# Sigmoid attention and a token mixer on one core: nearly all matrix work in 64x64 tiles, with the PSUM banks and the order of steps written out

## The chip, the core and the metric

The kernel runs on one core of one Trainium2 chip. A core has five engines with an instruction queue each: TensorE (PE, matrix products, with weight loads shown apart as PEld), VectorE (DVE), ScalarE (ACT), GpSimd (POOL) and SyncE (SP, which here issues the DMAs). TensorE writes into PSUM, eight banks of 512 float32 for each of 128 partitions; VectorE and ScalarE copy from there to SBUF. The metric is the time of one execution in microseconds of the device.

## The reference

```python
scores = scale * np.matmul(q, k.transpose(0, 1, 3, 2)) - np.log(S)
attn = 1.0 / (1.0 + np.exp(-scores))
attn_out = np.matmul(attn, v)                  # batch 8, 12 heads, 448 tokens, 64 wide
x = attn_out.transpose(0, 2, 1, 3).reshape(B, S, H * D)        # 8 x 448 x 768
wq = x @ w_q                                    # 768 -> 64
wk = x @ w_k
W_tok = scale * np.einsum('bsd,btd->bst', wq, wk)
mixed = np.einsum('bst,btd->bsd', W_tok, x)
out = np.maximum(mixed, 0.0) @ w_out            # 768 x 768
```

Inputs and output are float32; the products run in bfloat16 with float32 sums.

## The kernel before

**Units.** Four heads of one batch are a quad: 24 quads, three to a batch. Tokens are split into seven groups of 64 (`NI`, `NP`). Two batches are a window; their output rows are computed together.

**Attention.** For each quad, q and k are loaded, cast to bfloat16 and transposed so that the 64-wide head lies along the partitions. There are several ways to do that, and a letter for each: small 64x64 transposes on TensorE (`q`, `k`), whole 128x128 ones (`a`, `b`), or transposes of 32x32 blocks on VectorE after GpSimd has swapped quarters of the tile (`c`, `d`, `arrange`), or VectorE alone (`r`, `s`, `z`, `quadrants`). A step `S` (`scores`, L329 is its sigmoid) makes the scores of one token group of the keys, in four 64x64 tiles and two PSUM banks, and ScalarE turns them into attention weights. A step `P` (`values`) multiplies these with v and sums over the seven groups in two banks; after the seventh, the sum is copied to the x tile `xt` (L351).

**Mixer.** `x` transposes a quad of x to token rows (`tr_x`, small or whole), `W` adds one of six parts of the wq and wk product (`mlp_wqk`), `N` transposes wk (`mlp_wkn`), `U` forms the wk-x product (`mlp_tmp`, or `mlp_tmp_tiled`), `M` the mix and its ReLU (`mlp_mix`). With `mlp_mix` associated this way, no 448x448 token matrix is formed.

**Output.** `O` is a part of an output block. In windows 1 and 2 (`TW`) it is `out_pair`: two token groups of 64, 48 products in 64x64 tiles, four parts, two banks. In windows 0 and 3 it is `out_chunk`, with whole 128x128 products of a token pair into one bank, or `out_halves`. The tiled blocks need w_out in both halves of the partitions; the second copy is made by DMAs from SBUF to SBUF (`C`, L920). `D` issues the store of a finished block.

**What sets the order.** The order is written out: `PLAN` is a string with one letter for each step, and every engine's instructions stand in its queue in that order, under `manual_schedule`. Loads are issued on SP in the order of `ORDER`, at most six ahead of the casts; GpSimd casts them in that order, except those marked for VectorE, which wait `LAG` score steps. Some loads wait for a given product (`BEHIND`). PSUM banks come from a list of free pairs, first in, first out (`bank2`, `bank1`, `release`). All four 64x64 tiles of a group run in TensorE together; where the next group has another tile shape, the shape changes. Letters `F` are dummy products of 128x512 in the first quads.

Of the kernel before, what the change touches and what calls it, by code (L numbers as in the profile page):

```python
# [9 lines left out]
F32 = mybir.dt.float32  # L10
# [7 lines left out]
def kernel(  # L18
# [49 lines left out]
    free2 = [0, 1, 2, 3]  # L68
    halves = []

    def bank2():
        n = free2.pop(0)
        return n, pairs[n], pairs16[n]

    def bank1():
        if halves:
            n, b = halves.pop(0)
        else:
            n, b = free2.pop(0), 0
            halves.append((n, 1))  # L80
        return (n, b), pairs[n][:, b], pairs16[n][:, b]

    def release(fb):
        if isinstance(fb, int):
            free2.append(fb)
        elif (fb[0], 1 - fb[1]) in halves:
            halves.remove((fb[0], 1 - fb[1]))
            free2.append(fb[0])
        else:
            halves.append(fb)  # L90
# [5 lines left out]
    spare = singles.tile([P, 8], F32)  # L96
# [3 lines left out]
    xts = [singles.tile([P, 2, 512], BF16, name=f"xt{n}") for n in range(2 * NJ)]  # L100
    wqks = [singles.tile([P, 512], BF16, name=f"wqk{n}") for n in range(2)]
    wq2s = [singles.tile([P, S], BF16, name=f"wq2{n}") for n in range(2)]
# [25 lines left out]
    def xt(u, j):  # L128
        return xts[u % 2 * NJ + j]


    TW = (1, 2,)
# [3 lines left out]
        "FSSFFFFKSSSqFFSSkFFSSDPpSFpPSPPPqSSkPSPPSSpPpPSabSXSPpSSPSPr"  # L136
        "PXpSPSSFSszSWWWWXSPWWPSppPNSpPSqkSSUSXSMSPpSMPpSppPSSqkSPpPP"
        "SPSWWcPSPXSWWSSdMWXSWSPpPpSpNPPSqSkSUSxSMSPpppSppSCPoSOSMSOo"
        "SqCkSOoCMSpPpSDpPcPSPSdoOSSocOSLLDLSXSdLLSLPPpSppPSPSoOSoSNC"
        "xSOcDSUSPPDSPprCdPpSPpSsPpPDPSPSoPSXoSMSOoSzLLxSLLLLScSoXoSM"  # L140
        "ppDpSPpDCSpdPSOOcSpppSpPSPPSONMSYOSxSOdOSpPpPpSSDPPoOSxSUcSL"
        "LLDdSSLLLppPSppPPSoSoMSOcSOSDdPpPPSPMoPSoPmOSOScdOoSxoSDOSON"
        "oSxSOOSSUpSppPSMcpPpLLLSLpPSPdLLpDDPPSOpoSxoSOmocDSoMSodooDS"
        "NOSoSOSPPPPDtcpSppOoSMoSODoSoSdMOOSPPScpppPSOPmoOSoxoDSdOSoS"
        "OLLSLLLSLoSooNxScoPppxSpdPSPPoSODDSoSOSOOSxoSOSTppPpPSpPpPpP"
        "mPppmmWWWWWWyyINiiitiiIMiiMMIiioOoOoOOoOoOoOOOO"
    )
    PLAN = "".join(PLAN)
    KIND = ["a"] + [t for t in PLAN if t in "qacer"]
# [6 lines left out]
    def arrange(n, eng):  # L156

        arranged.add(n)
        if KIND[n] in "er":
            return  # L160
# [21 lines left out]
    def load1(n, nm, eng, m):  # L182
        u, j = quads[n]
        if KIND[n] in "cer" and nm != "v":
# [19 lines left out]
    def cast1(n, nm, e):  # L204
        if KIND[n] in "cer" and nm != "v":
# [48 lines left out]
    moves = []  # L254

    def move():
        n, m = moves.pop(0)
        for g in range(2):
            for h in range(2):
                own, other = 64 * g + 32 * h, 64 * g + 32 * (1 - h)  # L260
                nc.sync.dma_start(
                    out=qk[n][other : other + 32, h].rearrange("p t i n -> p (t i n)"), in_=m[own : own + 32, 1 - h],
                )

    def tr(n, nm, kind):
# [9 lines left out]
        if kind in "cdef":  # L275
# [5 lines left out]
            if kind in "ef":  # L281
                if t == 0:
                    moves.append((n, p_mv.tile([P, 2, 2 * S], BF16, tag="mv", name="mv")))
                nc.vector.transpose(out=moves[-1][1][:, t].bitcast(F32), in_=w)
# [5 lines left out]
        if kind in "abh":  # L290
            transposes_whole(ps[:, t], t16, slice(0, NI))
        else:
            transposes(ps[:, :, t * S : (t + 1) * S], t16, slice(0, NI))
# [41 lines left out]
    def values(n, i, tail, eng):  # L335
# [10 lines left out]
        if i == NI - 1:  # L346
            if tail:
                for h in range(2):
                    COPY["vs"[h]](out=xt(u, j)[:, h, 0:S], in_=ps[:, h, 0:S])  # L349
# [621 lines left out]
```

## Time and profile before

| what | value |
|---|---|
| median of 3 runs | 185.96 us (185.79 to 186.71) |
| span of the profiled execution | 184.0 us |
| own time of that execution beside its span | not given on the page; the median is 1.96 us above the span |
| TensorE busy | 174.7 us, 3662 products |
| ScalarE busy | 162.7 us, 168 of its 209 instructions are sigmoids |
| VectorE busy | 133.1 us |
| GpSimd busy | 124.3 us |
| moved by DMA | 48.51 MB, 264 GB/s mean |

How to read the profile: an engine's busy time is the union of its instructions' times. Products on TensorE overlap, and their ends are modelled, so a busy TensorE is not one at its peak. In a row of the timeline, the first number is the start in microseconds from the start of the span, the second the time from the first start to the last end of a run of like instructions, `xN` their count. In a view by stretches, each engine has its busy time and, in brackets, the instructions that ended there; PEclk is the share of its full clock that TensorE was granted. In a view of groups, the busy time and the mean length in ns stand behind the bar, then the idle time before them and what ended it. In a view of waits: total us, times, longest.

### The profile page before, as it was taken

Reading aid. Unit: us, or ns where it says so; the run is one execution under the profiler, and the core shown is the slowest. Engines: PE = TensorE matmul, PEld = TensorE weight load, DVE = VectorE, ACT = ScalarE, POOL = GpSimd, SP = SyncE. Lnnn points to the kernel's source line nnn. Section 1 sums busy time; section 2 is a strip of 40 time slices with the busy share of each in tenths; the row PEclk is TensorE's granted clock in tenths of the full one; section 3 lists DMA queues with packets and bytes.
Section 4 is the critical chain, followed back from the end, with each engine's and each line's share of the span. In section 5 each row is a group of like instructions: output and inputs, shape, how many; then the busy total and the mean of one; then the engine's idle time right before and its main releaser. Section 6 shows DMA issues by size and latency. Waiting matters only on the chain.

```text
span 184.0 us, 8547 instructions
## 1 busy us (share of the span) xinstructions
PE 174.7 (95%) x3662; PEld 115.3 (63%) x3662; DVE 133.1 (72%) x209; ACT 162.7 (88%) x209; POOL 124.3 (68%) x171
## 2 busy tenths in 40 slices
PE   7888989999999999999999999999999999999990
PEld 7344545554545464565555778667898878869660
DVE  3334878788798887899797788587678476686820
ACT  4699999999999999999999989999999989876230
POOL 1458799995799899779999996999999920000000
PEclk9999999999999999999999999999999999999998
DMA  5999999969999999989987984798997443422596
GB/s 177 356 385 383 328 361 360 379 229 304 331 357 326 298 289 332 344 291 315 337 298 232 349 284 145 221 321 226 352 309 226 106 125 89 116 62 60 133 237 171
DMA packets 26085, 48.51 MB, mean 264 GB/s; under 512 B 3968, under 2 KB 19968, under 8 KB 26048
## 3 DMA queue, kind: packets, MB, share of 16 engines
q1 hardware_dynamic: 25888, 47.79, 79.9%
q8 instruction: 28, 0.46, 1.1%
q10 hardware_dynamic: 160, 0.20, 0.4%
q14 instruction: 9, 0.07, 0.1%
HBM read 35.78 MB, written 11.01 MB: 254 GB/s over the span
## 4 chain that ended last, share of the span: by engine, by line
PE 78%; ACT 14%; issue 3%; DVE 2%; ACTq 0%
PE banks L119 73%; ACT at L329 13%; PE banks L122 6%; DVE xt L351 1%; DVE mx L480 1%; ACTq L661 0%; DVE ld L680 0%; DVE wqk L426 0%; ACT xt L349 0%; ACT wq L428 0%; ACT ld L678 0%; DVE zeros L716 0%; ACTq L329 0%; ACTq L678 0%; ACTq L428 0%
## 5 line engine op out<-in xcount | busy, mean ns | idle before, releaser
L329 ACT ACTIVATE at<-banks 128x896 bf16<-128x896 f32 x168 | 141.2, 932 | 4.8 <-PE banks L119 4.3
L119 PE MATMUL banks<-wout,mx 64*64 64x384 bf16 (+2 forms) x954 | 68.5, 323 | 0.0
L119 PE MATMUL banks<-qk 64*64 64x448 bf16 x672 | 61.8, 358 | 2.0 <-ACT at L329 1.3
L119 PEld LDWEIGHTS <-mx 64*64 64x64 bf16 (+1 forms) x954 | 41.1, 105 | 14.4 <-issue 5.1
L119 PE MATMUL banks<-at,v 64*64 64x448 bf16 x672 | 45.6, 351 | 0.2
L119 PEld LDWEIGHTS <-qk 64*64 64x64 bf16 x672 | 25.5, 105 | 21.4 <-issue 12.6
L209 POOL CAST qk<-ld 128x896 bf16<-128x896 f32 x28 | 33.6, 1210 | 5.4 <-DVE qk L280 1.4
L119 PEld LDWEIGHTS <-v 64*64 64x64 bf16 x672 | 22.7, 106 | 9.2 <-issue 2.4
L351 DVE CAST xt<-banks 128x896 bf16<-128x896 f32 x19 | 20.7, 1088 | 10.2 <-PE banks L119 9.8
L480 DVE TENSOR_SCALAR mx<-banks 128x1024 bf16<-128x1024 f32 (+2 forms) x21 | 21.1, 1011 | 3.9 <-PE banks L119 3.1
L219 POOL CAST v<-ld 128x896 bf16<-128x896 f32 x23 | 21.6, 954 | 1.9 <-DMA ld<-in_v_dram 1.6
L168 POOL COPY qk<-qk 32x448 uint32<-32x448 uint32 x28 | 16.4, 587 | 1.6
L280 DVE STREAM_TRANSPOSE qk<-qk 128x448 f32<-128x448 f32 x28 | 17.4, 629 | 0.0
L171 POOL COPY qk<-swap 32x448 uint32<-32x448 uint32 x28 | 15.9, 568 | 1.6
L165 POOL COPY swap<-qk 32x448 uint32<-32x448 uint32 x28 | 15.7, 562 | 1.7
L560 DVE COPY o<-banks 128x768 f32<-128x768 f32 x11 | 10.5, 952 | 5.7 <-PE banks L119 4.1
L122 PEld LDWEIGHTS <-xt 64*64 64x64 bf16 (+1 forms) x528 | 10.9, 107 | 3.6 <-issue 2.4
L119 PE MATMUL banks<-xt,wqk 64*64 64x448 bf16 (+1 forms) x138 | 12.7, 350 | 0.1
L122 PE MATMUL banks<-ident,xt 64*64 64x64 bf16 (+1 forms) x528 | 12.4, 198 | 0.1
L395 DVE COPY xn<-banks 128x1024 bf16<-128x1024 bf16 (+1 forms) x14 | 9.0, 648 | 3.3 <-PE banks L122 2.7
L119 PE MATMUL banks<-wqk,tmp 64*64 64x256 bf16 (+1 forms) x72 | 8.9, 298 | 0.1
L119 PE MATMUL banks<-wq,tmp 64*64 64x256 bf16 (+1 forms) x72 | 9.0, 300 | 0.0
(73 smaller groups left out, 159.1 us busy)
## 6 DMA issues: line engine op xcount, KB each, us to landing
ld<-in_q_dram SPq DMA_DIRECT2D x24, 448.0 KB, 5.8
ld<-in_v_dram SPq DMA_DIRECT2D x24, 448.0 KB, 5.7
ld<-in_k_dram SPq DMA_DIRECT2D x23, 448.0 KB, 6.2
out_dram<-o SPq DMA_DIRECT2D x42, 192.0 KB, 4.8
ld<-in_moe_w_out_dram SPq DMA_DIRECT2D x6, 384.0 KB, 6.2
out_dram<-ld SPq DMA_DIRECT2D x11, 192.0 KB, 2.8
wout<-wout SPq DMA_DIRECT2D x12, 96.0 KB, 6.7
out_dram<-ld SPq DMA_DIRECT2D x4, 96.0 KB, 2.4
```

The source lines that it names most:

```text
L119: products.append(nc.tensor.matmul(*args, **kw))
L122: products.append(nc.tensor.transpose(*args, **kw))
L165: eng.tensor_copy(out=z[lo], in_=w[hi, 0])
L168: eng.tensor_copy(out=w[hi, 0], in_=w[lo, 1])
L171: eng.tensor_copy(out=w[lo, 1], in_=z[lo])
L209: COPY[e](out=f[:, :, "qk".index(nm)].rearrange("p e i d y -> p e y i d"), in_=ld.pop((nm, n)).rearrange("p (y i e d) -> p e y i d", y=2, ...
L219: COPY[e](out=t16.rearrange("p i b d -> p b i d"), in_=ld.pop((nm, n)).rearrange("p b (i d) -> p b i d", i=NI),)
L280: nc.vector.transpose(out=qk[n][:, t].rearrange("p t i n -> p (t i n)").bitcast(F32), in_=w)
L329: nc.scalar.activation(at, sc[:, :, 0:S], ACTF.Sigmoid, bias=attn_bias, scale=attn_scale)
L351: COPY[eng](out=xt(u, j)[:, :, 0:S], in_=ps[:, :, 0:S])
L480: nc.vector.tensor_scalar(dst, ps, moe_scale, 0.0, ALU.mult, ALU.max)
L560: COPY["s" if act else "v"](out=o, in_=ps[:, :, 0:NB])
```

## The change

- Every window is tiled: `TW` holds all four, and the output blocks are all `out_pair`, 28 blocks of 48 products. `out_halves`, `mlp_tmp_tiled` and the special last chunk are gone. The mixed tile `mx` holds 12 x 224 columns a batch instead of 12 x 256, without overlap; for that, wq is kept with 32 tokens of the other half beside it (`extended`, small extra copies), and the blocks of the middle token group of both batches are one block.
- x tiles are seven groups of 128 columns without padding, so the x transposes are 28 small or 7 whole ones a quad, instead of 32 or 8. Nine memsets of padding and seven of a spare tile are gone.
- The wk-x product is 28 tiles of 64x64 with 192 columns, in two banks, summed over the seven token groups.
- 18 quads instead of 16 are transposed on VectorE (four by `r`), five instead of seven on TensorE.
- PSUM banks are named by step in `BANKS`.
- `PLAN` and `ORDER` are new. `LAG` and `BEHIND` have no entries; casts on VectorE or ScalarE stand in `PLAN` as `1` and `2`. TensorE changes its tile shape 25 times instead of 84. The dummies are three groups of four 64x64 products (`E`).
- The last block is copied in halves by VectorE and ScalarE and stored by four DMAs on SP and four on ScalarE's queue (`store_last`).

```diff
+    BANKS = (
+        "abcd012301302113021330212012031e31231203200gh202101203c10321"
...
     def bank2():
-        n = free2.pop(0)
+        n = int(given.pop(0))
+        assert not held & {2 * n, 2 * n + 1}
+        held.update({2 * n, 2 * n + 1})
         return n, pairs[n], pairs16[n]
...
-    xts = [singles.tile([P, 2, 512], BF16, name=f"xt{n}") for n in range(2 * NJ)]
+    xts = [singles.tile([P, NI, 2, NP], BF16, name=f"xt{n}") for n in range(2 * NJ)]
...
-    TW = (1, 2,)
+    TW = (0, 1, 2, 3,)
...
-        "FSSFFFFKSSSqFFSSkFFSSDPpSFpPSPPPqSSkPSPPSSpPpPSabSXSPpSSPSPr"
...
-        "mPppmmWWWWWWyyINiiitiiIMiiMMIiioOoOoOOoOoOoOOOO"
+        "SSSKSSSqESkSSSSEDPqSkpSrPSSDPSpPPsSPSppSzXSSPPPSPSp1pcdS1pSp"
...
+        "PPPSlpSPPLSlSlplSpcdpLSpppPSSqkSxrSSxSXXSCpspSpSPpCPPSNSPSzU"
+        "PSPCpCrPPSSCPCsWwWSWSXWWSzPPSXSpPPPSNPSSMMSPSPppScMpPSPSSdUS"
+        "xMSPPSpPSxpPPSSwWWwxSWWcSPppSOSodppSOSPPoOSODNmODSODSODOcmoS"
...
+        "PLPMpPPmlLLxllxOoOyoNOOuOomOmomOOOoOOOOoooOoOOoOo"
...
             fb, _, ps = bank1()
+            for i in range(NI):
+                mt(ps[:, i * P : (i + 1) * P], xts[u % 2 * NJ + j][:, i].rearrange("p h n -> p (h n)"), ident16)
+            ps = ps[:, 0 : NI * P].rearrange("p (i g d) -> p g i d", i=NI, g=2)
+        else:
+            fb, _, ps = bank2()
+            for i in range(NI):
                 for g in range(2):
+                    for h in range(2):
                         mt(
+                            ps[HALF[h], g, i * NP : (i + 1) * NP], xt(u, j)[HALF[g], h, i],
                             ident16[HALF[g], HALF[g]],
                         )
...
+    def extended(u):
+
+        if u // 2 not in TW:
+            return slice(32, 32 + S), None, None
+        if u % 2:
+            return slice(0, 32 + S), slice(0, 32), slice(S // 2, S // 2 + 32)
+        return slice(32, 64 + S), slice(32 + S, 64 + S), slice(32 + S // 2, 64 + S // 2)
...
     def mlp_tmp(u, act):
+        tmps[u] = p_one.tile([P, 2, NJ * DH], BF16, tag="tmp", name="tmp")
+        fb, ps, _ = bank2()
+        for i in range(NI):
             for y in range(2):
+                for x in range(2):
                     mm(
+                        ps[HALF[x], y, 0 : NJ * DH], wkn[u][HALF[y], i, :], xns[u][HALF[y], NJ * x : NJ * x + NJ, i, :],
+                        start=(i == 0), stop=(i == NI - 1),
                     )
...
+        T = S // 2
+        begin = (0, 32 + T) if u % 2 else (32, 64 + T)
+        for x in range(2):
+            if w in TW:
+                for y in range(2):
+                    for z in range(2):
+                        mm(
+                            ps[HALF[z], x, y * T : (y + 1) * T], tmps[u][HALF[x], y, c * DH : (c + 1) * DH],
+                            wq[x][HALF[x], begin[z] : begin[z] + T], start=True, stop=True,
+                        )
...
+        def store_last():
+            for y in range(2):
+                for x in range(2):
+                    cols = slice(x * NB, (x + 1) * NB)
+                    dma = (nc.scalar if y else nc.sync).dma_start
+                    for u in us:
+                        dma(
+                            out=out[2 * w + u].rearrange("(r n i) d -> i r n d", r=2, i=NI)[NI // 2, y, :, cols],
+                            in_=o[64 * x + 32 * u : 64 * x + 32 * u + 32, y],
+                        )
...
-    LAG = 9
-    BEHIND = {("w", 1): 728, ("v", 8): 856, ("q", 22): 2264, ("v", 20): 2392, ("v", 23): 2648}
+    BEHIND = {}
...
         if t == "E":
+            fb, ps, _ = bank2()
             for g in range(2):
                 for h in range(2):
+                    mm(ps[HALF[h], g, 0:S], zeros[HALF[g], 0:NP], zeros[HALF[g], 0:S], start=True, stop=True)
+            release(fb)
+            continue
```

More of the change, by code (lines that the diff above doesn't have):

```diff
@@ L396, in tr_x @@
+        if tail:
+            for g in range(2):
+                COPY["vs"[g]](out=xn[:, g], in_=ps[:, g])
+        else:
+            COPY[eng](out=xn, in_=ps)
         release(fb)
@@ L556, in out_pair @@
         if part < 3:
-            opened.append((w, blocks, part + 1, fb, ps))
+            opened.append((w, us, k, part + 1, fb, ps))
             return
-        o = o_tile([P, 2, NB])
-        COPY["s" if act else "v"](out=o, in_=ps[:, :, 0:NB])
+        late = len(cast) == len(ORDER) + 2
+        last = w == NU // 2 - 1 and len(us) == 2
+        o = ld_next()[:, 0:D].rearrange("p (b x) -> p b x", b=2) if late else o_tile([P, 2, NB])
+        if last:
+            for y in range(2):
+                COPY["vs"[y]](out=o[:, y], in_=ps[:, y, 0:NB])
+        else:
+            COPY["s" if act else "v"](out=o, in_=ps[:, :, 0:NB])
         release(fb)
-        (u0, i0), (u1, i1) = blocks
         def store():
@@ L625, in out_halves @@
+        stores.append((o_tiles[0] - 1, store_last if last else store))
+        if tail or late:
             flush()
```

438 lines of the change are left out of this document (138 added, 300 removed), and 10 rows, old and new, of the table ORDER.

## The prediction

> **What bounds the kernel now.** I read the parts of the page first: the busy shares, then the 40 slices.
>
> ```profile
> span 184.0 us, 8547 instructions
> PE 174.7 (95%) x3662; PEld 115.3 (63%) x3662; DVE 133.1 (72%) x209; ACT 162.7 (88%) x209; POOL 124.3 (68%) x171
> ACT  4699999999999999999999989999999989876230
> PEclk9999999999999999999999999999999999999998
> ```
>
> TensorE and ScalarE are both near full, so shares decide nothing. The second view is the busy time by stretches, cut where ScalarE begins the first sigmoid of a quad (four heads of one batch, seven sigmoids): quads 0 to 7, 8 to 15, 16 to 23, the tail, and what follows the last copies.
>
> ```profile
> core 0: us, PE busy (x) PEld busy (x) DVE busy (x) ACT busy (x) POOL busy (x), PEclk, DMA share, GB/s
> 6.20:52.60 46.40, 42.60 (x896) 23.02 (x892) 32.91 (x45) 45.91 (x56) 36.60 (x45) 1.00 0.98 342
> 52.60:102.70 50.10, 50.09 (x892) 28.04 (x885) 43.31 (x63) 49.45 (x63) 45.03 (x61) 1.00 0.94 311
> 102.70:161.00 58.30, 58.30 (x1524) 46.58 (x1520) 42.22 (x57) 54.91 (x68) 41.35 (x59) 1.00 0.71 217
> 161.00:180.40 19.40, 18.52 (x330) 13.28 (x322) 12.28 (x25) 9.93 (x21) 0.00 (x0) 1.00 0.52 128
> 180.40:184.00 3.60, 0.00 (x0) 0.00 (x0) 0.00 (x0) 0.00 (x0) 0.00 (x0) 0.77 0.55 161
> ```
>
> For a pace instead of a share I took the timeline.
>
> ```profile
> 8.33 16.41 ACT L329 ACTIVATE at<-banks 128x896 bf16<-128x896 f32 x20 [0.32 <-PE banks L119]
> ...
> 60.85 0.36 PE L119 MATMUL banks<-qk 64*64 64x448 bf16 x4
> 61.20 1.14 PE L119 MATMUL banks<-wout,mx 128*128 128x384 bf16 x6
> 62.26 0.57 PE L119 MATMUL banks<-qk 64*64 64x448 bf16 x8
> ...
> 64.95 0.62 PE L122 MATMUL banks<-ident,xt 128*128 128x128 bf16 x8
> ...
> 163.46 0.74 PE L122 MATMUL banks<-ident,xt 64*64 64x64 bf16 x64
> ...
> 166.97 1.72 PE L119 MATMUL banks<-wout,mx 64*64 64x384 bf16 x36
> ```
>
> Each row gives the start, the length of the whole run of instructions, and how many they are. Twenty sigmoids in 16.41 us, the last one 0.93 long: (16.41 - 0.93) / 19 = 0.815 us each, 5.70 a quad. For TensorE I take the row's time less one product's own length, over the count less one. Output products of 384 columns in 64x64 tiles: (1.72 - 0.32) / 35 = 0.040 us each, so four, which fill the array, take 0.161. Whole ones of 128x128: (1.14 - 0.33) / 5 = 0.162, the same. So the columns set the pace, 0.42 ns each in the whole array, and four tiles share it: 0.047 us for 448 columns in a tile, 0.027 for 256, 0.024 for 224, 0.020 for 192. A 64-column transpose takes (0.74 - 0.19) / 63 = 0.0087, a whole one (0.62 - 0.22) / 7 = 0.057. I price every product of the two instruction orders so.
>
> Quads 0 to 7 then hold 33.5 us of products and 37 changes of tile shape in 46.4 us, against 8 x 5.70 = 45.6 us of sigmoids: ScalarE sets the pace. Quads 8 to 15 hold 43.7 us and 42 changes, quads 16 to 23 hold 55.2 us and 2 changes, with less ScalarE work than the stretch takes: TensorE sets it.
>
> **The change, part by part.** Of 84 changes of tile shape 25 stay, all before the last score, where 81 were. The price of one comes from the rows at 60.85 to 62.26: four score products take 4 x 0.047 = 0.19, so the output products could begin at 61.04 and begin at 61.20: 0.16. Six of them take 0.98, to 62.18; the scores begin at 62.26: 0.08. That is 0.12 to 0.13 a change. Quads 8 to 15 agree: 43.7 + 42 x 0.13 = 49.2 of 50.1 us. Saved: 59 x 0.13 = 7.7 us of TensorE time.
>
> The products themselves, in us: x transposes, 448 small and 80 whole, become 504 and 42, 8.5 to 6.8; output blocks, 816 small and 138 whole, become 1344 small, 54.4 to 54.2; the wk-x product 4.8 to 4.5 and the mixes 4.9 to 4.5; q and k transposes, less the two quads that go to VectorE, 4.5 to 3.2; dummies 2.4 to 0.6; wk transposes 64 to 112, +0.4. Sum -5.3. TensorE loses 13 us of work. This is worth what the stage that it leaves is bound by.
>
> The output blocks also move. Before, they start in quad 8. After, all need the tiled layout and both copies of w_out, whose last casts are issued in quad 9 and copies in quad 10, and the order puts the first block at the end of quad 12. So TensorE's work by stage is: quads 0 to 12, 756 products of 448 columns, 18 whole ones, 506 small and 42 whole transposes and 164 others, 49.5 us, and 25 changes, against 13 x 5.70 = 74.1 us of sigmoids; quads 13 to 20, 744 output products (30.0 us), 492 of 448 columns (23.1), 172 wk-x and mix products (3.8) and 238 transposes (2.1), 58.9 us and no change, against 56 sigmoids (45.6 us) and about 9.5 us of copies on ScalarE; quads 21 to 23, 17.3 us against 17.1.
>
> - Quads 0 to 12: ScalarE's pace. The saving in TensorE work is idle time. I take 5.74 a quad, between the sigmoids' own 5.70 and the 5.80 of before (46.4 / 8): 74.6 us.
> - Quads 13 to 23: TensorE's pace. Quads 16 to 23 of before, priced 55.2 + 2 x 0.13 = 55.5, (672 output products, 476 of 448 columns, 356 others) took 57.4 from first to last score (row below), 1.035 times the price; by the sigmoids' own stretch, 58.3 / 55.5 = 1.05. I take 1.04: 76.2 x 1.04 = 79.3 us.
>
> ```profile
> 102.30:159.72 57.42, 57.42 (x1504) 1.00 0.72 221
> 159.72:180.40 20.68, 19.80 (x358) 1.00 0.52 126
> ```
>
> From the first sigmoid to the end of the last that is 153.9 us, where before took 46.4 + 50.1 + 58.3 = 154.8: a gain of 0.9. Bounds: 150.5 (quads 13 to 23 at the bare price, 5.70 a quad before) and 157 (1.06 and 5.80, and 1 for waits).
>
> - The tail after the last score. TensorE holds 18.7 us of priced products before, and 3 changes, 19.1 of the 20.3 between the last score at 159.7 and the last copy at 180.04 (row below). After it holds 20.3 and no change, because 372 output products are left, 7.75 of the 28 blocks, against 144 small and 54 whole ones. Chains there (last x copy, wq and wk sum, wk transposes, product, mix) are covered: the sum takes a ScalarE and a VectorE step of some 0.5 us each, and four parts of an output block, 4 x 0.48 us, stand between. I take 20.3 x 1.03 = 20.9, so +0.5; bounds -0.1 and +1.5.
> - The end. Before:
>
> ```profile
> 179.34 0.58 ACTq L661 DMA_DIRECT2D out_dram<-ld  x1
> 180.04 0.32 ACT L678 COPY ld<-banks 128x192 f32<-128x192 f32 x1 [1.79 <-PE banks L119]
> 180.39 0.50 ACTq L661 DMA_DIRECT2D out_dram<-ld  x1
> ```
>
> After, the last copy is of 384 columns (0.48 in this kernel's row of that size, +0.16), and the last store is four DMAs of 32 partitions on SP and four on ScalarE's queue, one behind the other, where one stood on each. At 0.35 to 0.5 us an issue the fourth starts 1.1 to 1.6 later, and what follows an issue, 184.0 - 180.39 = 3.6 us, stays. I take +1.5; bounds +0.5 (smaller pieces land earlier) and +2.0.
>
> ```profile
> L680 ACT COPY o<-banks 128x384 f32<-128x384 f32 x5 | 2.4, 482 | 0.1
> L209 POOL CAST qk<-ld 128x896 bf16<-128x896 f32 x28 | 33.6, 1210 | 5.4 <-DVE qk L280 1.4 <-POOL qk L171 1.3 <-POOL wq L417 0.9
> L280 DVE STREAM_TRANSPOSE qk<-qk 128x448 f32<-128x448 f32 x28 | 17.4, 629 | 0.0
> ```
>
> Costed at nothing: POOL's eight more q and k casts (1.2 each) and two w_out casts less four wqk and two other casts, some 7 us in all, hidden because its last work for q and k, at 128 of its 131 us of work, is due with quad 23, which starts after some 145; VectorE's twelve more transposes of 0.63 (7.5 us), paid for by fewer casts, copies and adds (about -14) and hidden in 42 to 43 busy of 50 to 58; the dropped memsets, the extension copies of 32 columns, the wider wk copies, off the path; banks named by step, where, from quad 13 on, a score that takes its predecessor's banks has 1.3 us or more of products ahead of it, a score's latency and its sigmoid. If POOL's cover is gone, SP is late next: see below.
>
> Sum against the profiled span: -0.9 + 0.5 + 1.5 = +1.1, 185.1 us. The page gives no other time for that execution; the median of the runs, 185.96, is 1.96 above its span, and I keep that: 187.1 us.
>
> [...]
>
> **The rivals.**
>
> 1. Not slower: TensorE does not bind quads 13 to 20, because its over-run of 4% belongs to before's order alone. Then the stretch of 13 to 23 takes 76.2 us or a little less, and quads 0 to 12 the bare 74.1: 150.3, a gain of 4.5, and the time is 183.5. It decides from the point where those two stages gain 2 us, which the tail and the end cost. For it: quad 8 to 15 ran within 2% of its price. Against: 16 to 23 did not.
> 2. A wait takes the place of the changes: the stores of quads 13 to 20 stand in SP's queue behind loads that wait for POOL's casts. POOL has some 61 us of work issued in a stretch of 61 us, where before was busy 45.0 of 50.1 at most. Three output buffers and a 4.8 us landing leave little room at a block each 2.9 us. The price is 2 to 4 us of TensorE waits, 189 to 191. For it:
>
> ```profile
> SPq L187 <- POOL qk L209: 12.7, 9, 2.9
> SPq L571 <- ACT o L560: 6.4, 3, 3.1
> out_dram<-o SPq DMA_DIRECT2D x42, 192.0 KB, 4.8
> ```
>
> SP waits for casts already. Against: VectorE's wait for a buffer appears nowhere in before.
> 3. The clock falls in quads 0 and 1, which lose their dummies: 4.4 us of products in 11.4, 39%, where before kept 62%. The trace shows half pace at its start:
>
> ```profile
> 2.77 1.81 PE L119 MATMUL banks<-zeros 128*128 128x128 bf16 x15
> ```
>
> (1.81 - 0.31) / 14 = 0.107 us against 0.057 later. At half pace quads 2 and 3 need 7.2 us each against 5.7: +1.5 to 3, so 189. [...] No stretch of before shows it: PEclk is 1.00 throughout.
>
> **How the numbers follow.** The forecast, 186.2 to 188.2, has 0.46; rival 1 0.24; rival 2 0.19; rival 3 0.11. Low is 183.5 (rival 1), high 190.0 (rival 2's middle), with about a tenth on each side. Its own range is 186.2 to 188.2. A measurement of this kernel tells 0.5%, 0.93 us, from no change: faster than 185.03 is most of rival 1, 0.22; within it, the rest and the forecast's lower edge, 0.2; slower 0.58.
>
> **What would show it.** Right: the first eight quads keep 5.70 to 5.76 us each with TensorE visibly idle; a stretch of some 79 us in which TensorE waits for nothing; the last sigmoid ending near 160; four issues on ScalarE's queue at the end, and a span that ends over 5 us behind the last product. Wrong: the last sigmoid ends before 157 (rival 1), VectorE or ScalarE waiting on a DMA for an output tile between 80 and 140 us (rival 2), PEclk under 0.95 before 25 us (rival 3).

## The result and the profile after

The changed kernel takes 200.62 us (median of four runs, 198.67 to 204.61), the one before 186.05 (185.79 to 186.71); 187.1 was forecast. The ratio is 1.069, 95% interval 1.064 to 1.073: slower by some 13 us. The ratio is formed from the two quickest runs of the change, at 198.7 and 198.9 us, while its only trace, shown here, is of the execution of 202.33 us.

The page of the changed kernel, its busy shares, two of its slice rows and the row of the queue that brings instructions:

```profile
span 200.5 us, 9696 instructions
PE 172.1 (86%) x4250; PEld 129.2 (64%) x4250; DVE 128.6 (64%) x192; ACT 163.2 (81%) x203; POOL 128.7 (64%) x175
PE   7668788879969975999999989789679999999990
ACT  3799999989969997499998978779769899995310
q8 instruction: 33, 0.54, 1.1%
```

TensorE is busy for 2.6 us less than before, ScalarE for 0.5 us more, and the span is 16.5 us longer. Both rows of slices have dips at about the same places. So no engine has much more to do; two engines stand still together. The stretches, cut at the first sigmoid, at the first one of quad 13, at the end of the last one and at the last copy, first after, then before (columns as in the forecast's table):

```profile
6.57:88.76 82.19, 66.63 (x1494) 39.71 (x1490) 60.23 (x88) 75.21 (x91) 65.81 (x82) 0.98 0.91 306
88.76:175.87 87.11, 80.96 (x2144) 66.62 (x2139) 56.44 (x79) 75.76 (x92) 61.53 (x86) 1.00 0.70 215
175.87:195.45 19.58, 19.49 (x582) 18.24 (x573) 9.68 (x18) 9.30 (x18) 0.00 (x0) 1.00 0.56 136
195.45:200.50 5.05, 0.00 (x0) 0.00 (x0) 0.47 (x1) 0.48 (x1) 0.00 (x0) 0.95 0.58 159
```

```profile
6.29:83.27 76.98, 73.16 (x1422) 39.98 (x1418) 59.87 (x83) 76.45 (x95) 63.34 (x80) 1.00 0.98 333
83.27:161.00 77.73, 77.73 (x1874) 57.65 (x1877) 58.57 (x81) 73.83 (x91) 59.64 (x84) 1.00 0.76 237
161.00:180.04 19.04, 18.52 (x330) 13.28 (x322) 12.24 (x25) 9.61 (x20) 0.00 (x0) 1.00 0.52 127
```

In quads 13 to 23 TensorE was busy for all of 77.73 us before and for 80.96 of 87.11 after: it waits, in the stretch where it was to wait for nothing. The view of waits of the changed kernel says for what (total, times, longest):

```profile
PE banks L122 <- issue: 10.2, 8, 3.0
ACT at L307 <- PE banks L122: 15.1, 19, 3.2
ACT o L530 <- DMA out_dram<-o: 1.8, 1, 1.8
DVE o L530 <- DMA out_dram<-o: 1.1, 1, 1.1
```

"issue" is a wait for nothing that the profile shows: no data, no bank, no other engine. The view of before has no such row for products. ScalarE's 15.1 us are the echo: sigmoids wait for scores. The timeline of TensorE shows one of these waits:

```profile
77.56 0.38 PE L122 MATMUL banks<-qk 64*64 64x448 bf16 x4
77.75 0.35 PE L122 MATMUL banks<-at,v 64*64 64x448 bf16 x1
80.40 0.92 PE L122 MATMUL banks<-at,v 64*64 64x448 bf16 x7 [2.30 <-issue]
```

It falls in the middle of eight like products, whose data are there. What sets the place is the count. Windows from the span's start to just ahead of the product that ends a wait, with the products that have run:

```profile
0.00:57.30 57.30, 44.92 (x991) 1.00 0.91 310
0.00:80.30 80.30, 63.33 (x1375) 1.00 0.89 296
0.00:108.70 108.70, 91.31 (x2015) 0.98 0.87 287
0.00:119.40 119.40, 101.28 (x2271) 0.99 0.87 289
0.00:128.80 128.80, 109.23 (x2527) 0.99 0.87 285
0.00:134.20 134.20, 114.06 (x2655) 0.99 0.86 285
0.00:146.60 146.60, 123.48 (x2911) 0.99 0.86 284
```

991, 1375, 2015, 2271, 2527, 2655 and 2911 are all 128n + 95. A product is two instructions, a weight load and a product, so 128 of them are 256 instructions, and the row q8 has 33 packets of 0.54 MB / 33 = 16 KB, where before had 28: 2 x 4250 / 256 = 33, 2 x 3662 / 256 = 28.6. TensorE gets its instructions in blocks of 256, and seven times in these rows the next block was not there. I call the time between two products' starts at these places a block gap where it is over 0.25 us: ten of them, 13.6 us in sum, 6.0 in quads 0 to 12 and 7.7 in quads 13 to 23 (before: four, 1.06 us, none over 0.3).

The single packets in the trace tell when. With nothing else in flight and products at full pace (the fetch by itself, below), a packet of that queue starts within 0.5 us of a block's start and lands 0.65 to 1.35 us behind it. In the changed kernel it starts 0.4 to 5.2 us behind the block's start and lands 1.4 to 6.5 us behind it; the first product of the next block never started sooner than some 1.3 us after the landing there. Less its gap, a block lasts 3.8 to 5.6 us in quads 13 to 23.

One more loss came behind a gap. TensorE's clock behind the gap of 2.65 us:

```profile
77.75:80.40 2.65, 0.35 (x6) 1.00 0.49 124
80.40:83.89 3.49, 3.49 (x60) 0.51 0.87 291
83.89:88.76 4.87, 4.87 (x108) 1.00 0.95 342
```

3.4 us at half pace are 1.7 us lost. The forecast's span and these two, 185.1 + 13.6 + 1.7, make 200.4; the span is 200.5. That they agree so well is in part luck: the end came 0.4 us under its term and the first sigmoid 0.3 us later than in before, and not every variant below adds up like this.

### The profile page after: what moved, and what is told of

Same layout as the page of the kernel before. It is cut to its first block, busy times and chain, and to the rows that moved or that the text cites. A ratio compares the mean times of both kernels' runs of the same rounds, so it can differ in the third digit from the quotient of the medians.

```text
span 200.5 us, 9696 instructions
## 1 busy us (share of the span) xinstructions
PE 172.1 (86%) x4250; PEld 129.2 (64%) x4250; DVE 128.6 (64%) x192; ACT 163.2 (81%) x203; POOL 128.7 (64%) x175
## 4 chain that ended last, share of the span: by engine, by line
PE 48%; DMA 16%; ACT 11%; DVE 9%; issue 9%; POOL 2%; SPq 1%; DVEq 0%; ACTq 0%; POOLq 0%
PE banks L122 45%; ACT at L307 10%; DMA ld<-in_k_dram 7%; DMA out_dram<-o 6%; PE banks L125 3%; DMA ld<-in_q_dram 3%; DVE mx L442 3%; DVE xt L330 2%; DMA out_dram<-ld 1%; DVE wqk L694 1%; DVE qk L272 1%; DVE o L530 1%; POOL v L222 1%; POOL qk L212 1%; DVE xn L359 1%
## 5 line engine op out<-in xcount | busy, mean ns | idle before, releaser
L307 ACT ACTIVATE at<-banks 128x896 bf16<-128x896 f32 x168 | 141.9, 944 | 16.7 <-PE banks L122 15.1
L122 PE MATMUL banks<-qk 64*64 64x448 bf16 x672 | 66.7, 360 | 9.2 <-issue 3.4
L122 PE MATMUL banks<-wout,mx 64*64 64x384 bf16 x1344 | 71.1, 323 | 2.1 <-issue 2.1
L122 PE MATMUL banks<-at,v 64*64 64x448 bf16 x672 | 50.7, 356 | 5.0 <-issue 3.9
L122 PEld LDWEIGHTS <-mx 64*64 64x64 bf16 x1344 | 49.8, 107 | 5.3
L212 POOL CAST qk<-ld 128x896 bf16<-128x896 f32 x36 | 42.2, 1191 | 14.3 <-issue 5.7
L122 PEld LDWEIGHTS <-qk 64*64 64x64 bf16 x672 | 30.3, 106 | 26.0 <-issue 16.9
L442 DVE TENSOR_SCALAR mx<-banks 128x896 bf16<-128x896 f32 (+1 forms) x20 | 18.8, 949 | 10.3 <-PE banks L122 10.1
L359 DVE COPY xn<-banks 128x896 bf16<-128x896 bf16 x21 | 12.8, 616 | 9.4 <-PE banks L125 8.4
L530 DVE COPY ld<-banks 128x768 f32<-128x768 f32 x9 | 8.6, 955 | 7.3 <-PE banks L122 6.5
L252 DVE STREAM_TRANSPOSE qk<-qk 32x448 f32<-32x448 f32 x16 | 10.2, 636 | 0.4
```

Source lines behind the costliest of these rows:

```text
L122: products.append(nc.tensor.matmul(*args, **kw))
L212: COPY[e](out=f[:, :, "qk".index(nm)].rearrange("p e i d y -> p e y i d"), in_=ld.pop((nm, n)).rearrange("p (y i e d) -> p e y i d", y=2, ...
L307: nc.scalar.activation(at, sc[:, :, 0:S], ACTF.Sigmoid, bias=attn_bias, scale=attn_scale)
L442: nc.vector.tensor_scalar(dst, ps, moe_scale, 0.0, ALU.mult, ALU.max)
L530: COPY["s" if act else "v"](out=o, in_=ps[:, :, 0:NB])
```

## The experiments

Theory F: the time is lost to fetches of instructions that come late because they stand behind other DMA traffic. Its rival, theory S, is the forecast's second one: waits for output buffers, stores and GpSimd's casts. "Gaps" are the block gaps of the profiled execution. Ratios are to the kernel before; the changed kernel's is 1.069 (1.064 to 1.073).

**Shifted blocks.** Do the waits follow the count or the step?

```diff
 mm(ps[HALF[h], g, 0:S], zeros[HALF[g], 0:NP], zeros[HALF[g], 0:S], start=True, stop=True)
+for _ in range(5):
+    mm(ps[HALF[h], g, 0:16], zeros[HALF[g], 0:NP], zeros[HALF[g], 0:16], start=True, stop=True)
```

> The changed kernel with 20 tiny products (16 columns) added to each of its three groups of dummies, in quads 0 and 1, where TensorE is idle anyway: some 1 us of work, and every later step moves by 60 products against the blocks of 128. Theory F: the gaps over 0.3 us lie at products 128n + 96 again, so at other steps than in the changed kernel, and the time can fall anywhere between 192 and 204 us. Theory S: the waits stay at the same steps (the same output blocks and quads), 198 to 201 us.

Measured: 200.37 us, ratio 1.075 (1.067 to 1.082), gaps of 12.7 us. Counted as above:

```profile
0.00:86.20 86.20, 72.10 (x1503) 0.92 0.84 278
0.00:98.00 98.00, 82.84 (x1759) 0.93 0.84 282
0.00:109.30 109.30, 93.37 (x2015) 0.94 0.84 282
0.00:129.90 129.90, 111.59 (x2527) 0.95 0.85 280
0.00:151.10 151.10, 130.60 (x3039) 0.95 0.84 279
```

Again 128n + 95, with all later steps moved by 60 products: the waits follow the count. The time lies in both expected ranges and decides nothing; the places do, since theory S had the waits stay at their steps. With the tiny products there was also a stretch at half clock, from 10.2 to 20.4 us, which I had not asked for.

**Shorter loads.** The loads of q, k and v from quad 4 on (q and k of quad 3 too) bring 4/7 or 2/7 of their bytes; 4/7 shown.

```diff
-    out=t, in_=SRC[nm][u, 4 * j : 4 * j + 4].rearrange("h (p r) d -> (h p) (r d)", r=2 * NI),
+    out=t[:, 0 : 8 * HD],
+    in_=SRC[nm][u, 4 * j : 4 * j + 4].rearrange("h (p r) d -> (h p) (r d)", r=2 * NI)[:, 0 : 8 * HD],
...
+c = slice(0, NI * HD if n < 4 else 4 * HD)
...
-    out=t,
+    out=t[:, :, c],
...
-    ),
+    )[:, :, c],
```

> The changed kernel, but from quad 4 on each load of q, k and v brings only 4/7 of its bytes (the rest of the buffer keeps older data, so the values are not the reference's); every product, copy and store stays. Theory F: a fetch waits behind fewer bytes, the gaps at products 128n + 96 fall from 13.4 us to under 2, and the time to 185 to 188 us, which is what the forecast gave without such gaps (187.1). Theory S: stores land somewhat sooner, casts on GpSimd last as long as ever: 193 to 198 us, with gaps that do not fall on those products.

> The changed kernel with 2/7 of the bytes of each load of q, k and v from quad 4 on, in place of 4/7 (188.65 us, gaps of 2.45 us) or all (200.6, gaps of 13.6): the values are not the reference's, every product, copy and store stays. Theory F: gaps under 1 us, time 186 to 188: that is what this order of instructions costs with its instructions in time, and the forecast's sum (187.1) is right but for the fetches. If more than the fetches was forecast wrong, the time stays above 188.5 with the gaps gone.

Measured: 188.65 us, ratio 1.013 (1.007 to 1.019), with 4/7 and gaps of 2.45 us; 188.33, ratio 1.012 (1.007 to 1.017), with 2/7 and gaps of 2.0 us. Both lie a little above theory F's times and gaps (2.0 us is twice the bound set) and far below theory S's (193 to 198 for the first). The second one's two stages:

```profile
6.08:81.71 75.63, 64.66 (x1494) 38.62 (x1496) 60.55 (x88) 74.83 (x91) 65.37 (x82) 1.00 0.58 167
81.71:162.06 80.35, 79.61 (x2144) 66.95 (x2138) 56.93 (x79) 75.45 (x92) 61.77 (x86) 1.00 0.52 136
```

Same products, same copies, same GpSimd work as after, and 13.3 us less in the two stages, with 0.58 and 0.52 of the DMA engines in place of 0.91 and 0.70. Less their gaps (0.7 and 1.3) they are 74.9 and 79.05, where the forecast had 74.6 and 79.3. That is, nearly, the change without late fetches: it is still no faster than before.

**A fetch by itself.** Products of zeros and loads, nothing else.

```diff
+until(96 + 3 * 128, NB)
+until(96 + 7 * 128, 16)
+at = 9
+for loads in (1, 2, 3, 4, 5, 6):
+    m = 128 * at + 96 - 30 - 11 * loads
+    until(m + 4, NB)
+    for _ in range(loads):
+        load(m)
+    at += 3
```

> None of the computation: TensorE alone with products of zeros in 64x64 tiles. First 480 of 384 columns, then 512 of 16 columns, then 384 columns again, and 1, 2, 3, 4, 5 and 6 loads of 448 KB issued just ahead of product 128n + 96 of every third block. Only a piece of the output is written. Theory F: a fetch takes 1.3 to 2 us with no load ahead of it and about 1.2 us more for each load; a block of 384 columns lasts 5.2 us, so with up to two loads there is no gap, from three on there is one of about 1 us more for each load, 4 us with six. The blocks of 16 columns, 1 us of work or little more, take about 3 us each: a fetch of 1.3 and some 1.4 until its first instruction starts. Theory S: the same pace with any number of loads, no gap at any product.

Measured, the timeline of TensorE:

```profile
1.18 23.07 PE L59 MATMUL banks<-zeros 64*64 64x384 bf16 x607 [1.18 <-DVE zeros L52]
24.96 1.20 PE L59 MATMUL banks<-zeros 64*64 64x16 bf16 x128 [0.71 <-issue]
28.69 1.88 PE L59 MATMUL banks<-zeros 64*64 64x16 bf16 x128 [2.53 <-issue]
32.69 1.88 PE L59 MATMUL banks<-zeros 64*64 64x16 bf16 x128 [2.12 <-issue]
36.14 95.72 PE L59 MATMUL banks<-zeros 64*64 64x16 bf16 x2304 [1.57 <-issue]
132.69 10.72 PE L59 MATMUL banks<-zeros 64*64 64x384 bf16 x257 [0.82 <-issue]
```

The first row ends at 607 = 128 x 4 + 95. Then short products run in lots of exactly 128 and stop, with no load in flight: 3.73, 4.00 and 3.45 us from lot to lot, of which 1.2 to 1.9 are work (with the clock at 0.5 to 0.7 there). So with nothing in the way of its fetch a block took some 3.5 us at least: there the packet lands 2.1 to 2.6 us behind the block's start, and the next block starts 1.25 to 1.5 us after that. From 36.14 on the products are of 384 columns again, 5.20 us a block, without a break until the six loads at its end: the wait ahead of 132.69 is the only one. For these blocks the packet lands so many us behind the block's start:

| loads of 448 KB just ahead | 0 | 1 | 2 | 3 | 4 | 5 | 6 |
|---|---|---|---|---|---|---|---|
| landing, us | 0.65 to 1.35 | 1.5 | 2.3 | 2.5 | 3.9 | 3.3 | 4.75 |

Each load costs some 0.5 to 0.75 us, half of what I had expected, and a gap (1.14 us) comes with six, not with three.

**Loads around a fetch.** Which loads delay it?

```diff
+at = 3
+for ahead in (100, 75, 50, 25, 0, -25, -50):
+    m = 128 * at + 96 - ahead - 45
+    until(m + 4, NB)
+    for _ in range(4):
+        load(m)
+    at += 3
```

> None of the computation: products of zeros in 64x64 tiles with 384 columns, 0.04 us each, and four loads of 448 KB at seven places: the last of the four is issued some 100, 75, 50, 25 and 0 products before product 128n + 96, and 25 and 50 products behind it. Only a piece of the output is written. If a fetch waits for what was issued before it (a queue in order), it is late with the loads 25 to 75 products ahead (3 to 4 us until it lands, as with four loads before: 3.9) and takes 1 us with the loads behind it. If the packets of all queues share the DMA engines in turn, it is late with the loads behind it as well, 2 us or more, and by about as much at every place.

Measured, for the seven places in turn: the packet lands 2.6, 3.2, 3.6, 2.4 and 2.2 us behind the block's start with the loads ahead of it or at it, and 1.0 and 0.9 us with the loads 25 and 50 products behind. (The next fetch, 5.2 us on, finds those loads in front of it and lands at 2.6 and 3.7.) So a fetch is late where packets of loads are running before it, and loads whose packets begin after it cost it nothing: in the last two places their first packets began 0.7 and 1.7 us behind the block's start, the fetch 0.2 us ahead of it.

A plain queue in order it is not, though. With the last of the four loads issued at the block's start, 1.79 of their 1.84 MB had not begun by then; the fetch landed at 2.2 us and the last of the loads' packets at 6.55. It passed most of what had been issued before it. Whether the packets take turns this run cannot tell, since in the last two places the fetch was on its way before any load.

The entries in `BEHIND` of the kernel before, 728, 856, 2264, 2392 and 2648, are all 128n + 88, eight products ahead of a block's start. In this run a load was issued 0.4 us behind the product it waited for, and its first packet began 1.0 us after that. By an estimate from these, the held loads' packets begin some 1.1 us behind the block's start, when an undisturbed fetch has about landed. The change emptied that list.

**The kernel before without its held loads.**

```diff
-BEHIND = {("w", 1): 728, ("v", 8): 856, ("q", 22): 2264, ("v", 20): 2392, ("v", 23): 2648}
+BEHIND = {}
```

> The kernel before with its five held loads set free (BEHIND empty), nothing else altered. Theory F: gaps of TensorE of 0.5 to 3 us come up at products 128n + 96 of the blocks that those loads stood behind (n = 5, 6, 17, 18, 20), and the time is 188 to 193 us. Theory S: loads that start earlier cost nothing, 185 to 187 us.

Measured: 187.12 us, ratio 1.005 (1.002 to 1.009), gaps of 2.1 us against 1.06. The sign is that of theory F, but the time lies between the two ranges (185 to 187 and 188 to 193), and gaps came up at two of the five blocks alone (0.54 us at product 863, 0.81 at 2399). The held loads are worth some 1 us there, so the empty list by itself is not the 13 us.

**Smaller products in the kernel before.** Same columns, 672 products more, no held loads.

```diff
-mm(
-    ps[HALF[x], y, 0:NB], ...
+for z in range(2):
+    mm(
+        ps[HALF[x], y, 192 * z : 192 * z + 192], ...
```

> The kernel before without held loads (187.1 us) and with each of the 672 output products of windows 1 and 2 cut into two of 192 columns: the same columns, so the same work, in 672 products more; loads, copies and stores stay. In quads 16 to 23 a block of 128 products then has some 3.3 us of work, less than the 3.5 to 4.0 us that a fetch took per block with no other traffic. If the number of instructions makes the gaps: 17 blocks there of 4 to 5 us, 68 to 85 us in place of 58, and a time of 197 to 217 us. If only the order of the loads does: 187 to 190 us.

Measured: 206.08 us, ratio 1.108 (1.101 to 1.115), gaps of 19.3 us. Quads 13 to 23 of this kernel and, below, of its base, the kernel before without held loads:

```profile
83.82:181.95 98.13, 83.70 (x2545) 65.94 (x2548) 58.80 (x81) 75.39 (x91) 59.61 (x84) 0.97 0.61 184
```

```profile
83.98:162.22 78.24, 77.77 (x1873) 58.05 (x1876) 58.62 (x81) 73.82 (x91) 59.61 (x84) 1.00 0.75 233
```

672 products more, no column more, 19.9 us more, at the same loads, stores and ScalarE, VectorE and GpSimd work. In this stage the gaps are 17 us more, and there are two stretches of 3.4 us at half clock. Six of the blocks that end in a gap last 3.6 to 4.0 us, gap included, about the pace of the fetch by itself. The number of instructions makes that loss.

**Fewer products in the changed kernel.** 36 products of 512 columns for 48 of 384.

```diff
-for b in range(3 * part, 3 * part + 3):
+for b in range((0, 2, 4, 6)[part], (2, 4, 6, 9)[part]):
...
-            ps[HALF[x], y, 0:NB], st, wout16[HALF[y], slot(y, b), x * NB : (x + 1) * NB],
-            start=(b == 0), stop=(b == 11),
+            ps[HALF[x], y, 0:512], st, wout16[HALF[y], slot(y, b), x * 256 : x * 256 + 512],
+            start=(b == 0), stop=(b == 8),
```

> The changed kernel with 36 output products of 512 columns for each block in place of 48 of 384: as many columns, so as much work for TensorE, in 336 products fewer (a quarter of the output's contraction is left out and some columns are made twice, so the output is not the reference's). Loads, copies, stores and their order stay. If the gaps come of too many instructions a microsecond for the fetch, a block of 128 products lasts about a fifth longer in quads 13 to 23, the gaps there fall from 7.7 us in sum to under 3, and the time to 191 to 195 us. If the gaps come of the loads alone, whatever the pace of the instructions, as many gaps of as many us stay and the time stays at 197 to 203 us.

Measured: 195.61 us, ratio 1.051 (1.045 to 1.057), just above the expected 191 to 195. The gaps of quads 13 to 23 are 4.4 us in place of 7.7, not under 3. The direction is theory F's again; with some 0.75 of the DMA engines busy a quarter fewer output products do not free every fetch.

**Loads held back in the changed kernel**, eight and eleven of them.

```diff
-BEHIND = {}
+BEHIND = {("k", 9): 600, ("k", 11): 856, ("v", 12): 1240, ("k", 19): 1880, ("k", 20): 2136, ("v", 19): 2392, ("k", 22): 2520, ("v", 21): 2776}
```

```diff
+BEHIND = {("q", 8): 472, ("k", 9): 600, ("k", 11): 856, ("q", 12): 984, ("v", 13): 1240, ("k", 19): 1880, ("q", 20): 2136, ("k", 21): 2392, ("q", 21): 2520, ("q", 22): 2648, ("k", 23): 2776}
```

> The changed kernel with eight loads held back until TensorE has done product 128n + 88 (k9, k11, v12, k19, k20, v19, k22, v21; n = 4, 6, 9, 14, 16, 18, 19, 21). Nothing else is altered. Theory F: TensorE takes its instructions in blocks of 256 (128 products), a block is fetched by one 16 KB packet that is asked for at product 128n + 96, and stands behind the loads in flight; the gaps at those products sum to 13.4 us in the changed kernel. With the loads put behind the fetch the gaps fall to under 5 us in sum and the time to 187 to 192 us. Theory S (stores and casts): the time is lost to waits for output buffers and for GpSimd's casts; loads that start later can only add to that: 198 to 202 us.

> The changed kernel with eleven loads held until product 128n + 88: those which were issued in the later half of a block, so that less stands ahead of the next fetch (q8, k9, k11, q12, v13, k19, q20, k21, q21, q22, k23 for n = 3, 4, 6, 7, 9, 14, 16, 18, 19, 20, 21). Theory F: the gaps at products 128n + 96 sum to under 4 us (13.4 in the changed kernel, 6 with the first choice of held loads, of which one, v12, then came 7 us late), the time 188 to 193 us. Theory S: 196 to 201 us, no better than the first choice.

Measured: 197.02 us, ratio 1.056 (1.049 to 1.063), gaps 6.5 us; 197.31 us, ratio 1.057 (1.051 to 1.063), gaps 8.1 us. Both miss theory F's times, and the second lies in the range set for theory S (196 to 201). Gaps in quads 0 to 12 fall from 6.0 to 1.4 and 2.2 us. One block shows how, the one that starts near 72 us. The loads and the copies of w_out that are issued around its start, first in the changed kernel, then with eight held loads:

```profile
69.91 1.15 SPq L198 DMA_DIRECT2D ld<-in_v_dram  x2
71.45 0.34 SPq L190 DMA_DIRECT2D ld<-in_q_dram  x1
71.84 5.83 SPq L815 DMA_DIRECT2D wout<-wout  x7
```

```profile
70.71 6.08 SPq L815 DMA_DIRECT2D wout<-wout  x8
76.89 1.07 SPq L198 DMA_DIRECT2D ld<-in_v_dram  x2
```

In the first its packet lands 6.5 us behind its start, and the gap of 2.65 us follows; in the second it lands at 2.1 us, and there is none. So three loads fewer in front make that difference, and not the copies of w_out. But v12 now came at 76.9 us in place of 69.9, and TensorE stood 1.15 us for values.

Quads 13 to 23 win less: gaps of 5.2 and 5.9 us for 7.7. The one at product 2527 grows from 1.6 to 2.0 and 2.8 us, and one of 1.5 and 2.8 us opens at 2399. What is moved off one fetch can lie in front of the next, as in the run of seven places.

**Four loads ahead in place of six.**

```diff
-if len(ring) >= 6 and ring[-6] not in cast:
+if len(ring) >= 4 and ring[-4] not in cast:
```

> The changed kernel with at most four loads issued ahead of their casts in place of six. Theory F: a fetch finds at most four loads in front of it (with loads issued together in front of a fetch, three cost no gap at 5.2 us a block and six cost 1.1 us): gaps under 8 us in sum, and 194 to 199 us, less if the loads' later start costs nothing. If the stores and the copies of w_out in the queue matter as much as the loads, the gaps stay at 10 us or more, 198 to 204 us.

Measured: 198.24 us, ratio 1.064 (1.057 to 1.072), not clear of the changed kernel's and in both expected ranges. The gaps, 10.2 us, are those expected if other traffic matters as much: loads ahead are not all that stands in front.

**No early stores, and four output buffers.**

```diff
-stores.append((o_tiles[0] - 1, store_last if last else store))
+stores.append((o_tiles[0] - 1, store_last if last else store if late else lambda: None))
```

```diff
-p_o = pool("o", 3)
+p_o = pool("o", 4)
-while stores and stores[0][0] <= o_tiles[0] - 3:
+while stores and stores[0][0] <= o_tiles[0] - 4:
```

> The changed kernel without the stores of the output blocks up to the last load (some 20 blocks are computed and copied, but not written out); loads, products and copies stay. If stores make the fetches late: the gaps of quads 13 to 23 fall from 7.7 us to under 3, those of quads 0 to 12 stay at some 3 to 6, and the time is 190 to 194 us. If the loads alone do: gaps of 6 to 8 us in quads 13 to 23, 196 to 201 us.

> The changed kernel with four output buffers in place of three, and a store flushed for its buffer one block later. Theory S: the waits of ScalarE and VectorE for a store to land (7.1 and 4.8 us of the chain) go, 194 to 197 us. Theory F: those engines wait less, TensorE does not; gaps at products 128n + 96 stay at 10 to 16 us in sum, the time at 198 to 203 us.

Measured without the stores: 198.09 us, ratio 1.065 (1.059 to 1.071), not clear of the changed kernel's. The time is in the range set for the loads alone (196 to 201), the gaps of quads 13 to 23 are near what was set for the stores (under 3): neither expectation holds as a whole. By stages:

```profile
6.15:90.31 84.16, 68.53 (x1494) 40.33 (x1494) 60.70 (x88) 75.43 (x91) 65.81 (x82) 0.94 0.89 297
90.31:172.58 82.27, 79.81 (x2144) 66.81 (x2138) 56.84 (x79) 75.63 (x92) 61.62 (x86) 1.00 0.55 163
```

Quads 13 to 23 take 82.27 us for 87.11, with gaps of 3.4 us for 7.7: in these two executions over half of the gaps there go with the stores. Quads 0 to 12, in which no block is stored, had gaps of 6.3 us and three stretches at half clock (PEclk 0.94), and took 2.0 us more than in the changed kernel. With four buffers: 197.88 us, ratio 1.063 (1.059 to 1.066), just below theory F's range and above theory S's (194 to 197), not clear of the changed kernel's; gaps 9.8 us, where 10 to 16 were expected. The waits on `o` for a landing, 1.8 and 1.1 us, are gone from the view, and TensorE still waits for "issue", 6.9 us.

**The last block, and all remedies together.** The block of the middle token groups is made first among the last four, so the last store has four DMAs of 64 partitions; then this, the eleven held loads and four buffers in one.

```diff
+if u == NU - 1:
+    chunks.append((u // 2, (0, 1), 3))
 chunks.extend((u // 2, (u % 2,), k) for k in range(3))
-if u % 2:
+if u % 2 and u < NU - 1:
     chunks.append((u // 2, (0, 1), 3))
...
-last = w == NU // 2 - 1 and len(us) == 2
+last = w == NU // 2 - 1 and us == (1,) and k == 2
...
+dma(out=out[2 * w + 1].rearrange("(p i) d -> p i d", i=NI)[:, k + 4 * y, cols], in_=o[HALF[x], y])
```

> As the kernel with eleven held loads, and the block of the middle token groups is no longer the last one, so the last store is two DMAs on SP and two on ScalarE's queue, of 64 partitions, in place of four and four of 32. If the row of issues sets the end, as in the forecast, two issues of 0.43 us less on each queue: 0.9 to 1.5 us less than the kernel with eleven held loads. If the landing of the last bytes sets it, within 0.3 us of it.

> The changed kernel with the eleven held loads, four output buffers and the plain last block together (196.0 to 197.9 us one by one). If their gains add: 192 to 195 us. If the fetches in quads 17 to 19 stay late whatever is done around them, 195 to 197.

Measured: 196.0 us, ratio 1.051 (1.046 to 1.056), 1.3 under the eleven held loads alone, but their intervals overlap, and the end itself says no. From this kernel (span 194.0) and, below, from the changed one (span 200.5):

```profile
189.04 0.48 ACT L528 COPY ld<-banks 128x384 f32<-128x384 f32 x1 [3.10 <-PE banks L122]
189.55 1.37 ACTq L552 DMA_DIRECT2D out_dram<-ld  x2
```

```profile
195.45 0.48 ACT L528 COPY ld<-banks 128x384 f32<-128x384 f32 x1 [3.10 <-DMA out_dram<-ld]
195.96 2.42 ACTq L553 DMA_DIRECT2D out_dram<-ld  x4
```

From the start of the last copy to the end it is 4.96 us against 5.05. The row of issues is 1.05 us shorter, and what follows it is 3.1 us in place of 2.1: the fewer, larger pieces took longer to land. All three together: 195.73 us, ratio 1.051 (1.044 to 1.058), gaps 5.3 us, of which 3.7 at products 2399 and 2527. The gains don't add, and no version of the change that does the whole work comes near the kernel before.

## Why the prediction was wrong, step by step

- **The direction** was right, the size was not: +1.1 us forecast, some +13 measured by the ratio, +14.6 by the medians. That it was right so clearly is luck: with 2/7 of the load bytes and less its 2.0 us of gaps the changed kernel comes to some 186.3 us, an estimate, which is hardly off before; the loss came of something that the sum did not have.
- **The step that failed** is the price of TensorE's work: "I price every product of the two instruction orders so", by columns alone. It was right as work, and it took for granted that a product which is small costs no more than its columns. 588 products more were counted as 5.3 us less. Nothing in the sum stood for the 256 instructions that must arrive for each 128 products, and the emptied list of held loads had no price. The page of before showed the queue that brings them (28 packets), and the entries of that list gave the period of 128. What the runs put in its place: 13.6 us of block gaps and 1.7 us at half clock. That the number of instructions is a cause of its own is shown by the kernel before with halved products (+19 us at equal work); that traffic in front of the fetches is the other one, by the shorter loads (ratio 1.069 to 1.012 at equal instructions), by the block near 72 us and by the loads around a fetch.
- **Quads 0 to 12**, forecast 74.6 us: 82.2, less gaps of 6.0 and the clock's 1.7, is 74.5. **Quads 13 to 23**, forecast 79.3: 87.1 less 7.7 is 79.4. As sums of a stage both were right; the price of a change of tile shape and the 1.04 were not measured apart.
- **The tail**, forecast +0.5: 19.58 for 19.04. **The end**, forecast +1.5: +1.1, within its bounds; but its reason, the row of issues, is not shown, since with half the issues the end came no sooner.
- **Rival 1** (TensorE doesn't bind) falls: without gaps the stretch of quads 13 to 23 takes 79 us, not 76.
- **Rival 2** had the right place and traffic and the wrong mechanism. Its sign did come: VectorE and ScalarE waited 1.1 and 1.8 us for an output tile to land, until 101.3 and until 121.2 us. But a fourth buffer took these waits away and left TensorE's. The stores go with late fetches: without them the gaps there are 3.4 us for 7.7. What the queue on SP costs was not tested by itself.
- **Rival 3** did not come in quads 0 and 1 of this execution (PEclk 1.00 there); the half clock came behind a gap. It can come: the kernel without early stores, whose first quads are the same, was at half clock from 8.0 to 11.4 us.
- **The weight loads**, which have no price in the sum, did not show: less its gaps, the stretch with most output products takes 79.4 us, as priced by columns, with weight loads beside them for 66.62 us (57.65 before).
- The sign that I named, "a stretch of some 79 us in which TensorE waits for nothing", is what showed the forecast wrong at first sight. The sign for quads 0 to 7, 5.70 to 5.76 us each, failed too: they took 47.6 us, 5.95 each, and 5.81 less their gaps. One bound is added wrongly, 76.2 + 74.1 being 150.3, as in rival 1, and not 150.5; nothing rests on it. The range, 183.5 to 190.0, held a spread for every known term and none for an unknown one.

What stays open: how the delay of a fetch adds up, in what turn its packet and those of loads are served, and why it reached 6.5 us in the full kernel with four loads in front, when four loads by themselves made it 2.2 to 3.9; why the kernel before, with 0.92 of its DMA engines busy from 122 to 141 us, keeps its gaps there at 0.3 us, and at 0.8 without its held loads; and why the variants of the changed kernel span 184.9 to 189.4 us less their gaps, of which the half clock explains a part only.

## What to carry to other kernels

Count TensorE's instructions, not its columns alone: cutting the same columns into smaller products leaves the fetch of the next block less time, and in the kernel before 672 products more, at equal columns, cost 19.9 us in quads 13 to 23. Divide the products of each stage by 128, set the stage's time per block against the landing time of the instruction queue's packets under that stage's DMA traffic (1.4 to 6.5 us in the changed kernel) and the 1.3 us until the next block starts, and look in the profile for waits put down to "issue" that recur at one remainder of the product count. Loads that can wait may be issued just behind a fetch; that was worth some 1 us in the kernel before and, by the ratios, some 2.4 in the changed one, and it can burden the next fetch (the gap at product 2527 grew from 1.6 to 2.0 and 2.8 us). A list of odd-looking dependencies in a tuned kernel is to be read as a cost before it is dropped.

## What the runs showed of the hardware

- TensorE's instructions came in blocks of 256, in one packet of 16 KB each (33 packets, 0.54 MB, for 4250 products and as many weight loads), and only about one block ahead: with no load in flight, short products ran in lots of 128 and stopped, 3.45 to 4.0 us from lot to lot. The gaps between blocks come to 13.6 us in the changed kernel and to 19.3 in the kernel of halved products, where the kernel before has 1.06.
- The packet was late where loads' packets were running before it: 0.5 to 0.75 us for each load of 448 KB that was issued in the 1 to 3.4 us ahead of the block. It did not wait for all that was issued before it (landed at 2.2 us, the loads at 6.55), and with no load's packet begun yet it landed in 0.9 to 1.0 us.
- Half the gaps of 2.5 us or more, seven of fourteen in the traces of the full kernels, were followed within 1.1 us by 3.4 us of TensorE at half its clock (PEclk 0.51 behind the gap of 2.65 us that began at 77.75); the other seven were not, among them the one of 3.3 us that ended at 146.7. What decides between the two these traces do not show.
- The times of four runs of the changed kernel (gaps of 13.6 us) lay 5.9 us apart, with eight held loads (6.5) 1.7, with shorter loads (2.45 and 2.0) 0.7 and 1.1; of the kernel before (1.06) four lay 0.9 apart and thirteen others 2.9. That the gaps make the spread is not shown.
